# A gated recurrence before an ELU MLP: chunks of 128 tokens with divided decays on half-array matmuls, in place of seven decay levels

## The chip, the cores and the metric

The kernel runs on one core of a Trainium2 chip. Its engines work side by side, each through its own list of instructions in a fixed order: TensorE (PE, with weight loads listed apart as PEld), VectorE (DVE), ScalarE (ACT), GpSimd (POOL) and SyncE (SP), which issues most transfers. The metric is the device time of one execution in microseconds (us). A profile is one such execution, recorded instruction by instruction.

## What is computed

A recurrence over 768 tokens for 4 batches of 8 heads (48 channels each), then an MLP with an ELU in the middle, all in float32. The weights arrive as float64.

```python
f = 1.0 / (1.0 + np.exp(-f_logit))
for t in range(S):
    state = f[:, :, t, :, None] * state + np.einsum('bhd,bhe->bhde', k[:, :, t], v[:, :, t])
    y[:, :, t] = np.einsum('bhd,bhde->bhe', q[:, :, t], state)
# y, with heads side by side, is x: 3072 tokens of 384
h = x @ w_in                                          # 2048 hidden channels
g = np.where(h > 0.0, h, np.exp(np.minimum(h, 0.0)) - 1.0)
out = g @ w_out
```

The gate logits have mean 2 and spread 0.5.

## The kernel before

The work is cut into 12 units of 256 tokens, three to a batch, each of two chunks of 128 tokens. Channels lie on the 128 partitions, two heads to a tile: head 2p in rows 0 to 47, head 2p + 1 in rows 64 to 111, zeros in between; four such pairs stand side by side.

**The recurrence by levels.** Inside a chunk, the score of a query at token i with a key at token j needs the product of all gates between them. `prepare(u)` (lines 171 to 198) turns logits into gates (L174 to L177: clamp, exponential, plus one, reciprocal, each on a 128x1024 tile), and puts the scores of each token with itself on the diagonal of the score tile `at` (L180, L185, L190, L192; `psD` is their PSUM tile). `level(u, l)` (lines 200 to 240) runs seven times per unit. At level l, blocks of 2**l tokens are paired: queries of the odd block meet keys of the even block. ACT copies the queries into a zero-padded tile `qz` (L212), TensorE makes scores of both heads (`psS`, L220), DVE and POOL multiply queries and keys by the next block's product (L230, L231), and DVE copies the scores under a mask into `at` (L233). All factors are products of gates, so none exceeds 1.

`chunk(u, c)` (lines 242 to 293) then makes the outputs: `psY` gets the state's part for both heads in one matmul (L262) and each head's part from `at` (L268, with 48 columns of v as weights). The keys are transposed (`psT`, L255) and multiplied with v into the state's increment `psU` (L276), and DVE carries the state on (L283, L286). ACT copies `psY` to `xt` (L272); six small transfers put the fourth pair's rows into the unused rows of the other three (L293).

**The MLP.** `mlp(u)` (lines 295 to 327) goes through 16 slabs of 128 hidden channels: three matmuls into `psH` (L303), two passes on ACT (L308, L309), one on DVE that finishes the ELU, here called the gate of the slab (L311), and two matmuls into the two `psM` tiles (L318), one slab later. A matmul in float32 stands as two records in the profile.

**The weights.** `weights(n)` (lines 120 to 166) loads one slab as float64 words and makes float32 of it: one pass on ACT (L146) and eight on DVE (L147 to L166), on 128x768 words.

**Order.** The Python program only says which work belongs to which step: MLP steps run two units behind the recurrence, two per level (L334 to L352), and all 16 slabs of weights are converted during units 0 and 1. A scheduler then fixes one order per engine by data dependences and the order of writing. Loads share the SP queue with the small transfers and the outputs.

Of the kernel before, what the change touches and what calls it, by code (L numbers as in the profile page):

```python
# [8 lines left out]
FP32 = mybir.dt.float32  # L9
# [7 lines left out]
def kernel(  # L17
    ctx: ExitStack,
    tc: tile.TileContext,
    q: bass.AP,  # [B, H, D, S]  # L20
    k: bass.AP,  # [B, H, D, S]
    v: bass.AP,  # [B, S, H * D]
    f_logit: bass.AP,  # [B, H, D, S]
    w_in: bass.AP,  # [H * D, DFF]
    w_out: bass.AP,  # [DFF, H * D]
    out: bass.AP,  # [B * S, H * D]
):
    """The gated recurrence, chunk by chunk of 128 tokens, and the ELU MLP on its outputs.

    Inside a chunk the decay between a key at j and a query at i > j is split at the start of the  # L30
    largest power-of-two-aligned block that holds i but not j. At level l (blocks of 2**l tokens)
    the even blocks give keys and the odd blocks queries:
        Q_l[i] = q[i] * prod(f[start of i's block .. i])
        K_l[j] = k[j] * prod(f[j + 1 .. end of j's block])
        T_l[n] = prod(f over block n)
    Each pair (i, j) belongs to exactly one level, and Q_l[i] . K_l[j] is its score. All factors are
    products of gates, so at most 1 in size: nothing is divided by a decay and nothing overflows,
    however small the gates are. Q_7, K_7 and T_7 carry the state from chunk to chunk.

    Channels lie on partitions, two heads to a tile: head 2p in rows 0..47, head 2p + 1 in rows  # L40
    64..111, zeros in between. The weights come as float32, or as the bits of float64 in int64.
    """
    nc = tc.nc
# [23 lines left out]
    # Queries of a level, the two heads of a pair next to each other, each on its own rows.  # L67
# [30 lines left out]
    # masks[l][j, n, w] = 1 where token j lies in block 2n, for the query (2n + 1) * 2**l + w  # L98
# [16 lines left out]
    # The rows of w_in in the order of the rows of xT: heads 2p and 2p + 1 of pair p < NKT, and the  # L115
    # heads of the last pair in the gaps, PAD rows to a gap.
# [212 lines left out]
    def run(steps, n):  # L329
        for _ in range(n):  # L330
            next(steps, None)
# [19 lines left out]
    for u in range(NU - LAG, NU):  # L351
        run(mlp(u), NFT + 2)  # L352
# [32 lines left out]
```

## Time and profile before

| | |
|---|---|
| median of 3 runs | 945.52 us (945.42 to 946.12) |
| span of the profiled execution | 943.6 us |
| TensorE busy | 830.0 us (88%), 4272 matmul records |
| VectorE busy | 543.6 us (58%) |
| ScalarE busy | 324.8 us (34%) |
| GpSimd busy | 186.6 us (20%) |
| bytes read and written in HBM | 31.46 MB, 4.72 MB |

The profiled execution has only its span recorded, 943.6 us; the median of the timed runs lies 1.9 us above it. Busy times of matmuls overlap each other, so distances from start to start tell the pace better than lengths. The chain that ended last gives TensorE 63% of the span, VectorE 16%, and 10% to issue. In a row of groups, the number after the bar is the busy time in us, then the mean of one in ns, then the engine's idle time just before, with what ended it.

### The profile page before, as it was taken

To read this page: it belongs to the slowest core of one execution; us is meant where nothing else is said; L and a number is where in the kernel's file an instruction comes from. 1 tells how busy PE (TensorE), PEld (TensorE's weight loads), DVE (VectorE), ACT (ScalarE), POOL (GpSimd) and SP (SyncE) were. 2 spreads that over 40 slices of the span, in tenths; PEclk is the share of its full clock that TensorE was granted. 3 is DMA by queue.
4 is the path that set the end of the run, shared out by engine and by line. 5 is a ranking of instruction groups with operands and counts; after the bars stand their busy time and mean duration, and the time that the engine had idled before them with its cause. 6 is when DMAs were issued, how large, how long until landed. Compare 5 with 4: busy or idle time off the path is not lost.

```text
span 943.6 us, 11405 instructions
## 1 busy us (share of the span) xinstructions
PE 830.0 (88%) x4272; PEld 644.1 (68%) x4272; DVE 543.6 (58%) x803; ACT 324.8 (34%) x661; POOL 186.6 (20%) x135
## 2 busy tenths in 40 slices
PE   1657657789799899899899899899999999999998
PEld 1555636567587677767777777777787887777775
DVE  8998999999843843742753753753542543421111
ACT  1323232344233433433433433423433433323332
POOL 4521411410310310220220220220211230100000
PEclk9767777999999999989999999989999999999999
DMA  9234514401100200201200200200100000000000
GB/s 219 57 109 110 130 45 124 104 1 46 43 1 22 68 1 21 69 0 26 63 1 19 71 1 18 72 1 17 55 1 3 20 1 22 1 1 22 0 17 17
DMA packets 33527, 38.10 MB, mean 40 GB/s; under 512 B 4160, under 2 KB 31424, under 8 KB 33472
## 3 DMA queue, kind: packets, MB, share of 16 engines
q1 hardware_dynamic: 33472, 37.37, 15.6%
q8 instruction: 34, 0.56, 0.2%
q14 instruction: 21, 0.17, 0.1%
HBM read 31.46 MB, written 4.72 MB: 38 GB/s over the span
## 4 chain that ended last, share of the span: by engine, by line
PE 63%; DVE 16%; issue 10%; POOL 2%; ACT 1%; DMA 1%; DVEq 0%; POOLq 0%; SPq 0%; ACTq 0%
PE psM L318 24%; PE psH L303 20%; PE psS L220 10%; DVE f L177 3%; PE psY L262 3%; PE psY L268 3%; DVE at L233 2%; PE psU L276 2%; DVE q L230 2%; DVE mlo L148 1%; DVE g L311 1%; POOL k L231 1%; DVE ex L158 1%; PE psT L255 1%; DVE ex L155 1%
## 5 line engine op out<-in xcount | busy, mean ns | idle before, releaser
L318 PE MATMUL psM<-wo,g 128*128 128x384 f32 x768 | 296.4, 510 | 35.0 <-DVE g L311 34.8
L303 PE MATMUL psH<-xt,wi 128*128 128x256 f32 x1152 | 286.8, 388 | 0.0
L303 PEld LDWEIGHTS psH<-xt,wi 128*128 128x128 f32 x1152 | 220.0, 196 | 53.9 <-issue 4.2
L318 PEld LDWEIGHTS psM<-wo,g 128*128 128x128 f32 x768 | 147.5, 197 | 105.1 <-DVE g L311 42.2
L220 PEld LDWEIGHTS psS<-qz,k 128*128 128x128 f32 x1344 | 179.8, 208 | 55.7 <-issue 23.1
L220 PE MATMUL psS<-qz,k 128*128 128x128 f32 x1344 | 185.0, 294 | 33.2 <-DVE at L233 18.7
L311 DVE SCALAR_TENSOR_TENSOR g<-e,psH 128x256 f32<-128x256 f32 x192 | 78.9, 416 | 227.4 <-ACT e L309 226.7
L233 DVE COPY_PREDICATED at<-mask,psS 128x512 f32<-128x512 int32 x168 | 144.8, 892 | 76.7 <-PE psS L220 76.5
L231 POOL TENSOR_TENSOR k<-k,tot 128x512 f32<-128x512 f32 x72 | 89.6, 1244 | 396.6 <-PE psS L220 333.5
L212 ACT COPY qz<-q 48x512 f32<-48x512 f32 x168 | 105.8, 630 | 178.3 <-PE psS L220 120.9
L308 ACT ACTIVATE e<-psH 128x256 f32<-128x256 f32 x192 | 73.5, 383 | 260.0 <-PE psH L303 253.0
L309 ACT ACTIVATE e<-e 128x256 f32<-128x256 f32 x192 | 79.9, 416 | 6.0
L177 DVE RECIPROCAL f<-f 128x1024 f32<-128x1024 f32 x12 | 78.5, 6546 | 0.1
L230 DVE TENSOR_TENSOR q<-q,tot 128x512 f32<-128x512 f32 x72 | 56.2, 780 | 3.6 <-ACT qz L212 3.5
L231 POOL TENSOR_TENSOR k<-k,f 128x512 f32<-128x512 f32 x12 | 18.6, 1551 | 199.7 <-PE psS L220 199.7
L262 PE MATMUL psY<-q,state 128*128 128x128 f32 x192 | 47.0, 328 | 9.3 <-DVE q L230 9.3
L185 PE MATMUL psD<-heads,qk 128*128 128x2 f32 x192 | 27.3, 273 | 28.1 <-POOL qk L180 23.4
L192 POOL TENSOR_TENSOR at<-ident,dots 128x2048 f32<-128x2048 f32 x12 | 43.4, 3618 | 38.1 <-ACT dots L190 38.1
L262 PEld LDWEIGHTS psY<-q,state 128*128 128x128 f32 x192 | 30.7, 199 | 24.8 <-issue 14.3
L185 PEld LDWEIGHTS psD<-heads,qk 128*128 128x128 f32 x192 | 27.5, 227 | 28.9 <-POOL qk L180 23.5
L268 PE MATMUL psY<-at,v 128*48 128x128 f32 x384 | 42.9, 303 | 0.7 <-DVE at L233 0.7
L283 DVE TENSOR_TENSOR state<-state,tot 48x192 f32<-48x192 f32 x40 | 15.3, 382 | 46.8 <-PE psY L262 46.3
(45 smaller groups left out, 390.0 us busy)
## 6 DMA issues: line engine op xcount, KB each, us to landing
raw<-in_moe_w_out_dram SPq DMA_DIRECT2D x16, 384.0 KB, 3.6
v<-in_v_dram SPq DMA_DIRECT2D x12, 384.0 KB, 4.9
raw<-in_moe_w_in_dram SPq DMA_DIRECT2D x32, 144.0 KB, 2.8
f<-in_f_logit_dram SPq DMA_DIRECT2D x24, 192.0 KB, 5.4
q<-in_q_dram SPq DMA_DIRECT2D x24, 192.0 KB, 3.4
k<-in_k_dram SPq DMA_DIRECT2D x24, 192.0 KB, 3.5
out_dram<-o SPq DMA_DIRECT2D x24, 192.0 KB, 2.0
raw<-in_moe_w_in_dram SPq DMA_DIRECT2D x32, 48.0 KB, 2.7
```

The source lines that it names most:

```text
L177: nc.vector.reciprocal(f[:], f[:])
L212: nc.scalar.copy(z[HALF[r], :, r, :].rearrange("p a (n w) -> p a n w", w=w), blocks(qt[HALF[r]], 1).rearrange("p (a n) w -> p a n w", n=n),)
L220: nc.tensor.matmul(pc[:, p], lhsT=kt[:, p, c * C : (c + 1) * C], rhs=z[:, p * NCU + c], start=True, stop=True,)
L230: nc.vector.tensor_tensor(out=blocks(qt[:], 1), in0=blocks(qt[:], 1), in1=total(0), op=ALU.mult)
L231: nc.gpsimd.tensor_tensor(out=blocks(kt[:], 0), in0=blocks(kt[:], 0), in1=total(1), op=ALU.mult)
L233: nc.vector.copy_predicated(out=at[:, c].rearrange("p a (n e w) -> p a n e w", e=2, w=w)[:, :, :, 1, :], mask=masks[l][:].unsqueeze(1).bro ...
L262: nc.tensor.matmul(py[:, p, :], lhsT=state[:, p, :], rhs=qt[:, p, cols], start=True, stop=False, skip_group_check=True,)
L303: nc.tensor.matmul(ph[:], lhsT=wi[:, kt, s * 128 : (s + 1) * 128], rhs=x[:, kt, :], start=(kt == 0), stop=(kt == NKT - 1),)
L308: nc.scalar.activation(e[:], ph[:], AF.Relu, scale=-1.0)
L309: nc.scalar.activation(e[:], e[:], AF.Exp, scale=-1.0)
L311: nc.vector.scalar_tensor_tensor(out=g[:], in0=e[:], scalar=-1.0, in1=ph[:], op0=ALU.add, op1=ALU.max)
L318: nc.tensor.matmul(pm[i][:], lhsT=g[:, i * 128 : (i + 1) * 128], rhs=wo[:, s - 1, :], start=(s == 1), stop=(s == NFT),)
```

## The change

The old kernel becomes a function `general` that runs only behind a flag. A new function `fast` does the same work in another way:

- **Divided decays.** With g = 1 + exp(-f_logit), the inverse gate, `prepare` forms the running product of g from the chunk's start (a scan on DVE, L496) and its reciprocal p (L499). Queries are multiplied by p (DVE, L502), keys by the running product (POOL, L503). One set of scores per chunk, set to zero above the diagonal (L529), replaces seven levels and the separate diagonal. Running products grow, so the largest of each chunk is compared with 2**60 (L505).
- **Half-array tiles.** Scores of the two heads use the 48 rows of each head (L524, two PSUM tiles). The increment of the state is made per head with 64 weight columns (L542), outputs with 48 columns (L565), and the state's part with 48 rows and 48 columns (L573). State tiles hold 48 columns per pair.
- **Conversion.** float64 becomes float32 with two passes on ACT (L462, L463), an integer sum on POOL (L471) and four on DVE (L464, L468, and L479 twice on half the words). L479 also turns values that are too small into zero.
- **Order.** The recurrence runs one unit ahead of the MLP, its steps laid out over the 16 slabs; the weights are converted inside the MLP of unit 0, one slab per step, with raw words fetched ahead into three buffers instead of two. `psM` comes two slabs after `psH`.
- **Flag and branch.** Comparisons of all chunks are gathered into one number, every engine loads it behind its last work of `fast` (L694), and `general` runs if any running product passed the limit (L695).

Names in the new lists: `gg` is the ELU's output, `bits`, `rnd` and `sq` are the words of a slab on their way, and `raw4` is the raw words of slab 4.

VectorE's order where weights are converted. Before, two slabs of the opening; the levels of unit 0 stand between their steps:

```order
L158 SCALAR_TENSOR_TENSOR ex2_271<-raw2_263,ex2_271 128x768
L233 COPY_PREDICATED at0_163<-mask5_133,psS0_5_0_355 128x16x32
L162 TENSOR_TENSOR wi_141<-mlo2_270,ex2_271 128x3x128
L166 TENSOR_TENSOR wo_142<-mlo2_270,ex2_271 128x384
L233 COPY_PREDICATED at0_163<-mask5_133,psS0_5_1_360 128x16x32
L147 TENSOR_SCALAR man3_305<-raw3_299 128x768
L151 TENSOR_SCALAR ex3_307<-raw3_299 128x768
L148 SCALAR_TENSOR_TENSOR mlo3_306<-man3_305,mlo3_306 128x768
```

Now, slabs 4 and 5 inside the MLP of unit 0:

```order
L464 TENSOR_SCALAR bits4_404<-raw4_371 128x768
L614 SCALAR_TENSOR_TENSOR gg0_3_464<-e0_3_461,psH0_3_457 128x256
L468 SCALAR_TENSOR_TENSOR bits4_404<-raw4_371,bits4_404 128x768
L479 SCALAR_TENSOR_TENSOR wi_106<-sq4_403,bits4_404 128x3x128
L479 SCALAR_TENSOR_TENSOR wo_107<-sq4_403,bits4_404 128x384
L614 SCALAR_TENSOR_TENSOR gg0_4_504<-e0_4_501,psH0_4_497 128x256
L464 TENSOR_SCALAR bits5_449<-raw5_396 128x768
L468 SCALAR_TENSOR_TENSOR bits5_449<-raw5_396,bits5_449 128x768
L479 SCALAR_TENSOR_TENSOR wi_106<-sq5_448,bits5_449 128x3x128
```

The conversion of a slab stands between the gates of the two slabs before it and of the slab itself, with nothing of a later slab in between; before, it stood among the levels, far ahead of the MLP.

TensorE's order in a later unit. Before, a level, some slabs and the start of a chunk:

```order
L318 MATMUL psM0_1_923<-wo_142,g0_10_1129 128x384
L220 MATMUL psS2_6_0_1166<-qz2_75,k2_71 128x128 x4
L220 MATMUL psS2_6_1_1171<-qz2_75,k2_71 128x128 x4
L303 MATMUL psH0_12_1182<-xt0_471,wi_141 128x256 x3
L318 MATMUL psM0_0_922<-wo_142,g0_11_1140 128x384
L318 MATMUL psM0_1_923<-wo_142,g0_11_1140 128x384
L303 MATMUL psH0_13_1193<-xt0_471,wi_141 128x256 x3
L255 MATMUL psT2_0_1215<-ident_104,k2_71 128x128 x4
L262 MATMUL psY2_0_1223<-q2_70,state0_143 128x128
L268 MATMUL psY2_0_1223<-at2_773,v2_171 48x128 x2
```

Now, the end of unit 3's recurrence inside the MLP of unit 2:

```order
L542 MATMUL psU3_1_1338<-v3_854,kn3_1_1289 64x48 x8
L606 MATMUL psH2_8_1350<-xt2_987,wi_106 128x256 x3
L624 MATMUL psM2_0_1228<-wo_107,gg2_6_1319 128x384
L624 MATMUL psM2_1_1229<-wo_107,gg2_6_1319 128x384
L565 MATMUL psY_104<-at3_1_1258,v3_854 48x128 x8
L573 MATMUL psY_104<-q0_69,state3_0_1245 48x128 x8
L606 MATMUL psH2_9_1388<-xt2_987,wi_106 128x256 x3
```

The pieces of a chunk now stand apart, each between whole slabs, and `psM` uses the gate of two slabs before. The core of the difference:

```diff
+    def convert(n):
+        nc.scalar.activation(rnd[:], lo, AF.Copy, scale=2.0**-29)
+        nc.scalar.activation(sq[:], raw[:].bitcast(FP32)[:, 1::2], AF.Square)
+        nc.vector.tensor_scalar(out=bits[:], in0=hi, scalar1=3, scalar2=0x3FFFFFF8,
+            op0=ALU.logical_shift_left, op1=ALU.bitwise_and)
+        nc.vector.scalar_tensor_tensor(out=bits[:], in0=hi, scalar=-(2**30), in1=bits[:],
+            op0=ALU.bitwise_and, op1=ALU.bitwise_or)
+        nc.gpsimd.tensor_tensor(out=bits[:], in0=bits[:], in1=rnd[:], op=ALU.add)
+        val = bits[:].bitcast(FP32)
+        for o, a, b in ((wi[:, :, n * 128 : (n + 1) * 128], sq[:, 0:DM], val[:, 0:DM]),
+                        (wo[:, n, :].unsqueeze(1), sq[:, DM:], val[:, DM:])):
+            nc.vector.scalar_tensor_tensor(out=o, in0=a..., scalar=(1.125 * 2.0**-15) ** 2,
+                in1=b..., op0=ALU.is_ge, op1=ALU.mult)
...
+    def prepare(u):
+        for h in range(2):
+            nc.scalar.activation(g[:, s], t["f"][:, s], AF.Exp, scale=-1.0)
+            nc.gpsimd.tensor_scalar_add(g[:, s], g[:, s], 1.0)
+            for p in (2 * h, 2 * h + 1):
+                for c in range(NCU):
+                    a = g[:, p, c * C : (c + 1) * C]
+                    nc.vector.tensor_tensor_scan(out=a, data0=a, data1=a, initial=1.0, op0=ALU.mult, op1=ALU.max)
+                    nc.vector.reciprocal(p_[:, p, c * C : (c + 1) * C], a)
+                nc.vector.tensor_tensor(out=t["q"][:, p], in0=t["q"][:, p], in1=p_[:, p], op=ALU.mult)
+                nc.gpsimd.tensor_tensor(out=t["k"][:, p], in0=t["k"][:, p], in1=g[:, p], op=ALU.mult)
...
+    def scores(u, c):
+        for p in range(HP):
+            for r in range(2):
+                nc.tensor.matmul(pc[r][:, p], lhsT=t["k"][HALF[r], p, cols], rhs=t["q"][HALF[r], p, cols], ...)
+        for r in range(2):
+            nc.vector.tensor_tensor(out=at[:, r], in0=pc[r][:], in1=causal[...], op=ALU.mult)
+    def advance(u, c):
+        nc.tensor.matmul(pu[FULL[r], p], lhsT=kns[u, c][:, p, FULL[r]], rhs=vts[u][:, c, h * D : (h + 1) * D], ...)
+    def outputs(u, c):
+        nc.tensor.matmul(py[HALF[r], p, :], lhsT=vts[u][:, c, h * D : (h + 1) * D], rhs=at[:, r, p], ...)
+        nc.tensor.matmul(py[HALF[r], p, :], lhsT=s[HALF[r], p], rhs=t["q"][HALF[r], p, cols], ...)
...
+    def attention(u):
+        return {0: [transposed(u, 0)], 1: [scores(u, 0)], 3: [advance(u, 0)], 4: [scores(u, 1)],
+                5: [] if last else [transposed(u, 1)], 6: [outputs(u, 0)], 8: [advance(u, 1)], 9: [outputs(u, 1)]}
...
+    for m in range(NU):
+        todo = attention(m + 1) if m + 1 < NU else {}
+        steps = prepare(m + 2) if m + 2 < NU else iter(())
+        for s in range(NFT):
+            T = m * NFT + s
+            for f in todo.get(s, ()):
+                f()
+            if m == 0 and ready < NFT:
+                if ready + 1 < NFT:
+                    fetch(ready + 1)
+                convert(ready)
+                ready += 1
+            up(T)
+            if T >= HLAG:
+                down(T - HLAG)
...
+        fast(tc, q, k, v, f_logit, w_in, w_out, out, flag)
+        seen = nc.values_load(flag[0:1, 0:1])
+        with tc.If(seen < 128):
+            general(tc, q, k, v, f_logit, w_in, w_out, out)
```

More of the change, by code (lines that the diff above doesn't have):

```diff
@@ L16, with general @@
 @with_exitstack
-def kernel(
+def general(
     ctx: ExitStack,
@@ L356, with kernel @@
+def kernel(tc, q, k, v, f_logit, w_in, w_out, out):
+    nc = tc.nc
+    with tc.tile_pool(name="flags", bufs=1) as pool:
+        flag = pool.tile([1, 1], I32, name="flag")
+        fast(tc, q, k, v, f_logit, w_in, w_out, out, flag)
+        seen = nc.values_load(flag[0:1, 0:1])
+        with tc.If(seen < 128):
+            general(tc, q, k, v, f_logit, w_in, w_out, out)
 _LAYOUT = {"q": (0, 1, 3, 2), "k": (0, 1, 3, 2), "v": (0, 2, 1, 3), "f_logit": (0, 1, 3, 2)}
```

251 lines of the change are left out of this document (added).

## The prediction

> **What bounds the kernel now.** I read the page's first two parts, then the table by stretches.
>
> ```profile
> span 943.6 us, 11405 instructions
> PE   1657657789799899899899899899999999999998
> DVE  8998999999843843742753753753542543421111
> PEclk9767777999999999989999999989999999999999
> ```
> ```profile
> 0.00:245.00 245.00, 164.94 (x844) 132.17 (x844) 232.28 (x314) 77.81 (x134) 74.99 (x61) 0.83 0.38 95
> 303.83:375.08 71.25, 66.77 (x363) 52.06 (x362) 38.51 (x56) 26.16 (x54) 14.31 (x9) 0.98 0.12 30
> ```
>
> Columns of the table: stretch, length, busy us of PE, PEld, DVE, ACT, POOL, PE clock, DMA share, GB/s. Until 245 us VectorE decides (232 of 245 us busy, PE clock 0.83). Then TensorE does, in a pattern of 71.25 us per unit (256 tokens), PE busy for 66.8. The timeline of PE gives the pace of the MLP alone and of a unit's parts:
>
> ```profile
> 860.39 1.46 PE L303 MATMUL psH<-xt,wi 128*128 128x256 f32 x6
> 861.69 1.45 PE L318 MATMUL psM<-wo,g 128*128 128x384 f32 x4
> 862.98 1.46 PE L303 MATMUL psH<-xt,wi 128*128 128x256 f32 x6
> ```
> ```profile
> 317.83 1.56 PE L318 MATMUL psM<-wo,g 128*128 128x384 f32 x4 [2.53 <-DVE g L311]
> ...
> 324.89 1.95 PE L220 MATMUL psS<-qz,k 128*128 128x128 f32 x16
> 326.68 1.84 PE L185 MATMUL psD<-heads,qk 128*128 128x2 f32 x16
> 330.47 2.61 PE L318 MATMUL psM<-wo,g 128*128 128x384 f32 x4 [1.95 <-DVE g L311]
> ...
> 362.18 0.60 PE L255 MATMUL psT<-ident,k 128*128 128x128 f32 x4
> 362.62 0.39 PE L262 MATMUL psY<-q,state 128*128 128x128 f32 x2
> 362.93 0.42 PE L268 MATMUL psY<-at,v 128*48 128x128 f32 x4
> 363.29 0.49 PE L262 MATMUL psY<-q,state 128*128 128x128 f32 x2
> 363.71 0.42 PE L268 MATMUL psY<-at,v 128*48 128x128 f32 x4
> ...
> 365.61 1.13 PE L276 MATMUL psU<-v,kn 128*128 128x96 f32 x8
> 366.58 1.49 PE L303 MATMUL psH<-xt,wi 128*128 128x256 f32 x6
> ```
>
> Start to start counts here, since ends overlap. A slab (128 hidden channels) takes 862.98 - 860.39 = 2.59 us, a unit of the MLP 16 x 2.59 = 41.4, all twelve 497: the floor that the change leaves alone. Of the other 30 us of a unit, seven levels of 2 x 16 score records (each matmul is two records) take 7 x 2 x 1.79 = 12.5, psU, psY and psT of two chunks some 9, and about 9 are gaps and slow starts like the two marked DVE.
>
> **What goes and what comes, per unit.** Levels, psD, the masked copies and the 1024-wide reciprocal in one piece go. There come, per chunk of 128, four transposes, 8 score matmuls on 48 rows, 8 psU with 64 columns, 8 outputs from `at` on 48 columns, and 8 from the state on 48 rows and 48 columns. Whether two half-array matmuls overlap decides their price. L268 already uses column halves; two narrow timeline windows show its four records:
>
> ```profile
> 652.10 0.32 PE L268 MATMUL psY<-at,v 128*48 128x128 f32 x2
> ```
> ```profile
> 652.25 0.28 PE L268 MATMUL psY<-at,v 128*48 128x128 f32 x2
> ```
>
> Two start together and the other two 0.15 later, so column halves run in pairs. Full-width records are 1.79/16 = 0.111 apart, so a pair costs 0.111. One round of psY (362.93 to 363.71, 0.78) is 2 x 0.111 for L262, two pairs 0.222, and 0.33 for two changes of shape: 0.165 a change. Row halves have no row here: between a pair (0.111 for two) and alone (0.222); nearest is L268, so I take the pair. The psD row bounds psU: 16 records with two columns moved still take the time of 128 columns, so loading 128 weight columns sets 0.11, and 64 columns about half of that. Per chunk:
>
> psT 0.44 (362.18 to 362.62); scores 8 x 0.111 = 0.89 (alone 1.78); psU 8 pairs at about 0.06 = 0.5 (alone 0.9); outputs from `at` 0.89; from the state 0.89 (alone 1.78); seven changes of shape 1.16. Sum 4.8, per unit 9.6. Units 3 to 11 pay this between slabs: 9 x 9.6 = 86, less 3 first chunks without a state (3 x 1.05) and 3 last without psT and psU (3 x 1.3): **79**. Alone in every case it is 130.
>
> **The opening.** The new order runs the recurrence of units 0, 1 and 2, then converts slabs 3 to 15 one by one inside the MLP of unit 0. VectorE's prices:
>
> ```profile
> L177 DVE RECIPROCAL f<-f 128x1024 f32<-128x1024 f32 x12 | 78.5, 6546 | 0.1
> L283 DVE TENSOR_TENSOR state<-state,tot 48x192 f32<-48x192 f32 x40 | 15.3, 382 | 46.8 <-PE psY L262 46.3
> L239 DVE TENSOR_TENSOR tot<-tot 128x256 f32<-128x256 f32 x12 | 5.0, 421 | 2.7 <-POOL k L231 2.7
> L239 DVE TENSOR_TENSOR tot<-tot 128x8 f32<-128x8 f32 x12 | 2.0, 165 | 0.2
> ```
> ```profile
> 56.00 0.94 DVE L158 SCALAR_TENSOR_TENSOR ex<-raw,ex 128x768 int32<-128x768 int32 x1
> ...
> 57.47 0.55 DVE L162 TENSOR_TENSOR wi<-mlo,ex 128x384 f32<-128x384 f32 x1
> ...
> 58.41 0.70 DVE L233 COPY_PREDICATED at<-mask,psS 128x512 f32<-128x512 int32 x1
> ...
> 59.48 0.55 DVE L151 TENSOR_SCALAR ex<-raw 128x768 int32<-128x768 int32 x1
> ```
> ```profile
> L180 POOL TENSOR_TENSOR qk<-q,k 128x1024 f32<-128x1024 f32 x12 | 29.8, 2485 | 16.7 <-DMA q<-in_q_dram 9.3 <-DVE heads L94 7.4
> ```
> ```profile
> 0.80 1.46 SPq L83 DMA_DIRECT2D v<-in_v_dram  x3
> 2.31 0.47 SPq L132 DMA_DIRECT2D raw<-in_moe_w_in_dram  x1
> 5.24 0.81 SPq L78 DMA_DIRECT2D f<-in_f_logit_dram  x2
> ```
> ```profile
> 10.34 1.28 ACT L175 ACT_TABLE_LOAD   x1 [10.34 <-DMA f<-in_f_logit_dram]
> ```
>
> Start: f lands at 10.3 behind three v loads and one of raw, 1.72 MB in 9.5 us. Now one v goes ahead: 0.93 MB, so about 7; then the table 1.3, half an exponential 0.5 and POOL's first sum 0.8 (by L180's rate): VectorE scans from 9.6. One prepare is 8 reciprocals (6546/1024 x 128 + 60 ns = 0.88 each, 7.0), 4 q products (0.42, 1.7) and 8 scans. A scan has no row: 0.17 (128x8) to 0.55 (a 768-wide operation); each element follows the one before, so 0.33, between them: 2.6. Together 11.3. A conversion is 0.55 + 0.94 + 2 x 0.55 = 2.6 on DVE. Up to slab 3's gate: three prepares 34, four conversions 10.4, twelve `at` at 0.70 = 8.4, nine state steps 3.4, four gates 1.7, together 58; plus waits for POOL's sum in each conversion (1.8 less what lies between, 1.4 x 4) and for the last score of a unit (3 x 0.6): 65. So **75 us** there.
>
> From then on VectorE's order is a ring: gate of slab n, two steps of n + 1, wait for POOL's sum, two products; only then can TensorE do psH of n + 1, ACT its two passes, and the next gate run. Nothing of slab n + 2 stands in between. Prices and hand-overs, from the timeline's end, and first a row of the old opening, where twelve psH records took 4.67 us against 12 x 0.216 = 2.6 at full clock:
>
> ```profile
> 105.10 4.67 PE L303 MATMUL psH<-xt,wi 128*128 128x256 f32 x12
> ```
> ```profile
> 937.62 0.42 ACT L309 ACTIVATE e<-e 128x256 f32<-128x256 f32 x1
> 937.65 2.45 PE L318 MATMUL psM<-wo,g 128*128 128x384 f32 x6
> 938.07 0.42 DVE L311 SCALAR_TENSOR_TENSOR g<-e,psH 128x256 f32<-128x256 f32 x1 [2.17 <-ACT e L309]
> 938.54 0.94 PEld L318 LDWEIGHTS psM<-wo,g 128*128 128x128 f32 x4 [0.70 <-DVE g L311]
> ```
>
> Gate 0.42, L464 0.55, L468 0.94, POOL 768/1024 x 2.49 = 1.8, first product 0.55, psH 1.46 at full clock or 2.8 at the slow one (2.0 taken, as the clock was 0.83 in the old opening and PE is now idle more), ACT 0.8, seven hand-overs of 0.05: 7.4. ACT's two conversions (at most 3 x 0.42 each, for three times the width) lie beside the DVE and POOL steps. Ten slabs at 7.4, slab 13 at 4.6 (the order starts its conversion before slab 12's gate), slab 15 at 5.9 up to psH: 84.5. The MLP of unit 1 starts at **160** (bounds 142 and 185: full clock, scans at 0.17 and no waits, or slow clock throughout, scans at 0.55 and 10 us more of waits).
>
> **The sum.** 160 + 1.3 (psM of the last slab) + 11 x 41.4 = 455 + 79 + 9 for what VectorE still holds up (in unit 1 it prepares units 3 to 6 as well: five slabs at 3.4 against 2.59 make 4; clock 2; the rest 3; bounds 0 and 25) + 3.5 (psM's end at 940.1 to the span's end) + 3 for flag and branch, which no row shows (bounds 0 and, as for a load of f, 5.4): 711. The median lies 945.5 - 943.6 = 1.9 above the span: **713 us**. The old gaps of 9 us a unit go because the 6.5 us reciprocal is cut into 0.88 us pieces, below the 2.5 us by which a gate may be late (three blocks of 1.3 until its psH buffer is wanted, less the 1.4 the gate takes). If that cover failed, 9 x 9 = 81 us would come back.
>
> **Rivals.** (1) Row halves do not pair: 130 for 79, 764. For it: no row of this kernel has row halves. Against: column halves pair. (2) Only the state outputs fail to pair, because both heads write the bank psY from different rows: 15 chunks x 0.89 = 13 more, 726. The Trainium skill, TensorEngine Tiling (Array Packing), § Restrictions and Gotchas, says that different row tiles cannot access the same PSUM bank at once; L268's halves share their rows, so no run here shows it yet. (3) A longer opening: slow clock all through adds 0.8 to twelve slabs, and 10 us of waits come before, 733; for it, the old opening's clock slices at 7 and 6. (4) A shorter one: full clock in the ring (12 x 0.54 = 6.5 less), scans at 0.17 (24 x 0.16 = 4 less), none of the 7 us of waits: 695. For it, the ring's longest pause of TensorE is only some 2.6 us. The Trainium skill, TensorE: Matmul & The Clock Gate, § Part 1, lets the clock fall only after an idle window of about 3.4 us, which by itself would make 706; the old opening's slices at 7 and 6 leave that open. (5) The other side, one mechanism: the end branch is taken. It decides at one chunk product of 1 + exp(-f) above 2**60; then the old kernel runs behind the new, 713 + 942 = 1655. Logits of mean 2 and spread 0.5 give 128 x 0.20 = 26 doublings, which speaks against it.
>
> **Chances.** Forecast 0.52, within 690 to 738; (1) 0.11, (2) 0.13, (3) 0.12, (4) 0.08, (5) 0.03, anything else 0.01. The range 686 to 766 takes in all but the branch and part of (1) and (4). A measurement here can tell about 0.2% from no change; only (5) is slower: faster 0.96, same 0.01, slower 0.03.
>
> **What would show it.** Pairs of L524, L542, L565 and L573 starting together and 16 records of L524 in about 0.9 us; one gate every 7.4 us between 75 and 150, VectorE's wait before L479 ended by POOL and before the gate by ACT; psH of unit 1 at about 160; units of 51 us after it; nothing on the branch's far side. Wrong would be a ring at another pace, 1.8 us for 16 scores, or gaps before psM as now.

## The result and the profile after

The changed kernel takes **707.75 us** (median of 4 runs, 707.47 to 709.7) against 945.82 us for the kernel before on the same chip: a ratio of **0.7469**, 95% interval 0.7441 to 0.7497. The forecast was 713 us, 686 to 766. The profiled execution has a span of 706.1 us. First the head of its page:

```profile
span 706.1 us, 9060 instructions
PE   0768844569999999999999999999999999999996
DVE  5889543438852722737124435471226221211110
PEclk9999898789999999999999999999999999999999
```

TensorE is full from about a quarter of the span on, where before it had fives to eights up to slice 9. VectorE is no longer full all through the opening: from slice 6 to 9 it has fours and threes, while TensorE has fours to sixes, so in that stretch no engine is full. The table by stretches says the same (columns as in the prediction: length, busy us of PE, PEld, DVE, ACT, POOL, PE clock, DMA share, GB/s):

```profile
0.00:75.00 75.00, 46.72 (x344) 33.75 (x345) 59.34 (x109) 18.74 (x30) 31.42 (x36) 0.96 0.65 137
75.00:160.00 85.00, 48.87 (x180) 27.13 (x178) 33.58 (x58) 30.80 (x52) 22.32 (x13) 0.87 0.38 105
160.00:205.00 45.00, 44.12 (x165) 32.02 (x166) 36.24 (x79) 17.35 (x42) 19.93 (x20) 0.96 0.53 117
205.00:664.00 459.00, 459.00 (x2589) 333.74 (x2588) 166.19 (x342) 151.04 (x357) 31.79 (x34) 1.00 0.10 29
```

Until 75 us VectorE is the busiest (59 of 75 us); from 75 to 160 no engine is busy for even 60% of the time; from 205 us TensorE has no gap at all. The stretch from 75 to 160 is the ring that the prediction described. One turn of it in VectorE's timeline, from one gate to the next:

```profile
83.60 0.42 DVE L614 SCALAR_TENSOR_TENSOR gg<-e,psH 128x256 f32<-128x256 f32 x1 [2.05 <-ACT e L612]
83.94 0.56 DVE L464 TENSOR_SCALAR bits<-raw 128x768 int32<-128x768 int32 x1
84.53 0.96 DVE L468 SCALAR_TENSOR_TENSOR bits<-raw,bits 128x768 int32<-128x768 int32 x1
87.49 0.56 DVE L479 SCALAR_TENSOR_TENSOR wi<-sq,bits 128x384 f32<-128x384 f32 x1 [2.01 <-POOL bits L471]
87.97 0.55 DVE L479 SCALAR_TENSOR_TENSOR wo<-sq,bits 128x384 f32<-128x384 f32 x1
90.57 0.42 DVE L614 SCALAR_TENSOR_TENSOR gg<-e,psH 128x256 f32<-128x256 f32 x1 [2.05 <-ACT e L612]
```

A turn is 90.57 - 83.60 = 6.97 us, of which VectorE waits 2.01 for POOL's sum and 2.05 for ScalarE. And a unit of TensorE behind the opening, cut to the pieces of the recurrence and what follows each:

```profile
254.54 0.60 PE L513 MATMUL psT<-ident,k 128*128 128x128 f32 x4
254.98 1.46 PE L606 MATMUL psH<-xt,wi 128*128 128x256 f32 x6
...
257.66 1.16 PE L524 MATMUL psS<-q,k 48*128 48x128 f32 x16
258.75 1.56 PE L606 MATMUL psH<-xt,wi 128*128 128x256 f32 x6
...
264.12 0.67 PE L542 MATMUL psU<-v,kn 128*64 128x48 f32 x16
264.72 1.56 PE L606 MATMUL psH<-xt,wi 128*128 128x256 f32 x6
...
274.40 1.08 PE L565 MATMUL psY<-at,v 128*48 128x128 f32 x16
275.41 1.08 PE L573 MATMUL psY<-q,state 48*48 48x128 f32 x16
276.42 1.56 PE L606 MATMUL psH<-xt,wi 128*128 128x256 f32 x6
...
305.39 0.60 PE L513 MATMUL psT<-ident,k 128*128 128x128 f32 x4
```

From psT to the next unit's psT are 305.39 - 254.54 = 50.85 us, where before a unit took 71.25; the MLP's 16 slabs are 41.4 of them.

### The profile page after: what moved, and what is told of

It reads as the page before. It is cut to its first block, busy times and chain, and to the rows that moved or that the text cites. A ratio compares the mean times of both kernels' runs of the same rounds, so it can differ in the third digit from the quotient of the medians.

```text
span 706.1 us, 9060 instructions
## 1 busy us (share of the span) xinstructions
PE 634.7 (90%) x3410; PEld 452.4 (64%) x3410; DVE 300.8 (43%) x599; ACT 229.3 (32%) x509; POOL 105.5 (15%) x102
## 4 chain that ended last, share of the span: by engine, by line
PE 72%; DVE 0%; ACT 0%; issue 0%
PE psH L606 32%; PE psM L624 30%; PE psS L524 3%; PE psY L565 3%; PE psY L573 2%; PE psU L542 1%; PE psT L513 1%; DVE g L496 0%; ACT o L631 0%; DVE gg L614 0%; PE psF L641 0%
## 5 line engine op out<-in xcount | busy, mean ns | idle before, releaser
L624 PE MATMUL psM<-wo,gg 128*128 128x384 f32 x768 | 283.7, 493 | 13.9 <-DVE gg L614 13.8
L614 DVE SCALAR_TENSOR_TENSOR gg<-e,psH 128x256 f32<-128x256 f32 x192 | 79.6, 414 | 320.6 <-ACT e L612 320.5
L624 PEld LDWEIGHTS psM<-wo,gg 128*128 128x128 f32 x768 | 146.3, 192 | 81.5 <-DVE gg L614 19.9
L499 DVE RECIPROCAL p<-g 128x128 f32<-128x128 f32 x96 | 85.2, 920 | 0.3
L503 POOL TENSOR_TENSOR k<-k,g 128x256 f32<-128x256 f32 x48 | 35.0, 746 | 225.4 <-DMA k<-in_k_dram 188.7
L496 DVE TENSOR_TENSOR_SCAN g<-g 128x128 f32<-128x128 f32 x96 | 39.4, 459 | 17.1 <-POOL g L492 17.1
L492 POOL TENSOR_SCALAR g<-g 128x512 f32<-128x512 f32 x24 | 35.4, 1491 | 67.7 <-ACT g L491 67.7
L471 POOL TENSOR_TENSOR bits<-bits,rnd 128x768 int32<-128x768 int32 x16 | 28.9, 1809 | 78.0 <-DVE bits L468 67.0
L524 PEld LDWEIGHTS psS<-q,k 48*128 48x128 f32 x384 | 29.2, 206 | 17.5 <-issue 11.3
L524 PE MATMUL psS<-q,k 48*128 48x128 f32 x384 | 36.5, 313 | 4.0 <-DVE q L502 2.6
L529 DVE TENSOR_TENSOR at<-psS,causal 128x512 f32<-128x512 f32 x48 | 30.9, 681 | 19.8 <-PE psS L524 19.8
L565 PEld LDWEIGHTS psY<-at,v 128*48 128x48 f32 x384 | 21.6, 129 | 13.2 <-issue 6.5
L565 PE MATMUL psY<-at,v 128*48 128x128 f32 x384 | 28.8, 291 | 0.7 <-ACT xt L577 0.7
L573 PE MATMUL psY<-q,state 48*48 48x128 f32 x320 | 22.4, 281 | 0.0
```

The costliest lines, as they stand in the source:

```text
L492: nc.gpsimd.tensor_scalar_add(g[:, s], g[:, s], 1.0)
L496: nc.vector.tensor_tensor_scan(out=a, data0=a, data1=a, initial=1.0, op0=ALU.mult, op1=ALU.max)
L499: nc.vector.reciprocal(p_[:, p, c * C : (c + 1) * C], a)
L503: nc.gpsimd.tensor_tensor(out=t["k"][:, p], in0=t["k"][:, p], in1=g[:, p], op=ALU.mult)
L524: nc.tensor.matmul(pc[r][:, p], lhsT=t["k"][HALF[r], p, cols], rhs=t["q"][HALF[r], p, cols], start=True, stop=True,)
L565: nc.tensor.matmul(py[HALF[r], p, :], lhsT=vts[u][:, c, h * D : (h + 1) * D], rhs=at[:, r, p], start=(p == 0), stop=first, skip_group_chec ...
```

## The experiments

The profiled span, and the ratio to the kernel before, which was measured beside each on the same chip. The runs were made on several chips, so it is the ratios that compare:

| kernel | median us | ratio (95% interval) | span us |
|---|---|---|---|
| changed kernel | 707.75 | 0.7469 (0.7441 to 0.7497) | 706.1 |
| e1 no branch | 703.39 | 0.7433 (0.7400 to 0.7466) | 702.6 |
| e2 halves in turn | 744.19 | 0.7853 (0.7808 to 0.7899) | 743.1 |
| e3 long conversion | 692.84 | 0.7319 (0.7275 to 0.7364) | 690.9 |
| e4 kernel before, short conversion | 940.10 | 0.9926 (0.9897 to 0.9955) | 938.2 |
| e5 slabs ahead | 721.62 | 0.7605 (0.7573 to 0.7637) | 720.0 |
| e6 slabs ahead, long conversion | 710.96 | 0.7491 (0.7460 to 0.7521) | 710.5 |
| e7 one reciprocal | 728.66 | 0.7666 (0.7628 to 0.7705) | 726.8 |
| e8 early flag | 720.34 | 0.7591 (0.7561 to 0.7621) | 718.8 |
| e9 ahead, f first | 688.72 | 0.7259 (0.7216 to 0.7302) | 686.6 |
| e10 ahead, f first, long | 687.02 | 0.7238 (0.7195 to 0.7280) | 683.9 |
| e11 or on VectorE | 695.85 | 0.7327 (0.7296 to 0.7359) | 693.0 |
| e12 ahead, or on VectorE | 683.84 | 0.7201 (0.7169 to 0.7233) | 681.9 |

**e1: the end.**

```diff
-        seen = nc.values_load(flag[0:1, 0:1])
-        with tc.If(seen < 128):
-            general(tc, q, k, v, f_logit, w_in, w_out, out)
```

> Left out: the reading of the range flag and the branch to the general kernel at the end; the flag itself is still worked out, and the order of everything else is unchanged. Theory (the changed kernel's span ends 6.1 us after its last psM, where before it was 3.5 us, and flag and branch make up the difference): 2.6 us less, 705 us for 707.8, and the span ends about 3.5 us after the last psM. Rival (the longer end is the output's transfer, which both kernels have, and the branch lies beside it): no change, 707.8 us, and still 6 us behind the last psM.

Measured: 703.39 us. In the changed kernel ScalarE's last copy starts at 700.04 and the span ends 6.1 us later; here it starts at 699.13 and the span ends 3.5 us later. So reading the flag and branching cost 2.6 us together in these two profiles, as the theory said, and the output's transfer alone, the rival, does not explain the end. (The ratios of the timed runs are too close to settle it by themselves.) The other 0.9 of the 3.5 us between the spans had been lost ahead of unit 3's first psT already (203.79 for 204.71).

**e2: do halves pair?**

```diff
-        for p in range(HP):
-            for r in range(2):
+        for r in range(2):
+            for p in range(HP):
```

(in `scores`, `advance` and twice in `outputs`)

> The same matmuls, but the loops over r and p change places in scores, advance and outputs: four matmuls on one half of the array, then four on the other, so that neighbours in the order share a half. Theory (halves overlap only with a neighbour on the other half): per chunk scores +0.89 us, psU +0.4, outputs from at +0.89, from the state +0.89, 3.07 us in all; 18 chunks of units 3 to 11 lie on the path, less three without a state and three without psU: 18 x 3.07 - 3 x 0.89 - 3 x 0.4 = +51 us, 759 us; 16 records of L524 take 1.8 to 2 us. Rival (a half costs about half of a whole matmul whoever its neighbour is): no change, 708 us, 16 records of L524 in 1.0 to 1.1 us.

Measured: 744.19 us, 37 us more by the spans for the 51 expected. The timeline of TensorE, one chunk's scores and one chunk's outputs:

```profile
268.19 1.71 PE L524 MATMUL psS<-q,k 48*128 48x128 f32 x16
...
286.29 1.55 PE L565 MATMUL psY<-at,v 128*48 128x128 f32 x16
287.77 1.55 PE L573 MATMUL psY<-q,state 48*48 48x128 f32 x16
289.25 1.56 PE L606 MATMUL psH<-xt,wi 128*128 128x256 f32 x6
```

The same 16 records take 1.63 us to the next start instead of 1.09 (scores), 1.48 instead of 1.01 (both kinds of output); psU takes 0.87 instead of 0.60. So the order of the halves decides, and the rival falls. The size was off by a third: four matmuls on one half are 0.111 apart, as pairs are, but where the half changes the first matmuls of the new half run beside the last ones of the old, and the change of shape is paid either way. Twice 1.75 us a chunk explains the unit (54.37 for 50.85); unit 3's first psT comes 7.5 us later as well (212.18 for 204.71), and the two together make the 37.

**e3: the old conversion in the new kernel.**

```diff
-        nc.scalar.activation(rnd[:], lo, AF.Copy, scale=2.0**-29)
-        nc.scalar.activation(sq[:], raw[:].bitcast(FP32)[:, 1::2], AF.Square)
...
-        nc.gpsimd.tensor_tensor(out=bits[:], in0=bits[:], in1=rnd[:], op=ALU.add)
...
+        nc.scalar.activation(mlo[:], lo, AF.Copy, scale=2.0**-52, bias=1.0)
+        nc.vector.tensor_single_scalar(out=man[:], in_=hi, scalar=0x000FFFFF, op=ALU.bitwise_and)
...
+        nc.vector.tensor_tensor(out=wo[:, n, :], in0=mlo[:, DM:], in1=scale[:, DM:], op=ALU.mult)
```

(lines 146 to 166 of the kernel before in place of lines 459 to 482)

> The changed kernel with the old eight-step conversion of a slab on VectorE, without POOL's sum and without the two passes of ACT for it (one in their place). VectorE's work per slab goes from 2.6 to 5.9 us. Theory (from 75 to 160 us a ring of waits through VectorE, TensorE and ACT sets the pace, of which VectorE's own work is less than half; in this order the first four steps of the next slab stand ahead of the gate, where VectorE waits anyhow): gates 6.3 to 7.4 us apart for 6.94 now, and up to slab 3 four conversions at +1.9 us: between -1 and +15 us, 707 to 723 us. Rival (the opening is VectorE's work and every microsecond of it counts, as in the kernel before): 16 x 3.3 = +53 us, 761 us, with VectorE's waits in the ring as long as now.

Measured: **692.84 us, 15 us faster** than with the short conversion. Both forecasts missed: the rival's sign, and the theory's range. VectorE's timeline in the ring's place:

```profile
106.85 0.41 DVE L617 SCALAR_TENSOR_TENSOR gg<-e,psH 128x256 f32<-128x256 f32 x1
107.19 0.55 DVE L473 TENSOR_SCALAR ex<-ex 128x768 int32<-128x768 int32 x1
107.77 0.96 DVE L476 SCALAR_TENSOR_TENSOR ex<-raw,ex 128x768 int32<-128x768 int32 x1
...
109.24 0.55 DVE L485 TENSOR_TENSOR wo<-mlo,ex 128x384 f32<-128x384 f32 x1
109.71 0.55 DVE L465 TENSOR_SCALAR man<-raw 128x768 int32<-128x768 int32 x1
...
111.98 0.42 DVE L617 SCALAR_TENSOR_TENSOR gg<-e,psH 128x256 f32<-128x256 f32 x1
```

A turn takes 5.13 us here with no wait in it: the scheduler put four steps of the next slab (L465 to L470) ahead of the gate, where they fill the time of psH and ScalarE. The eight steps are 4.8 us start to start (107.19 to 111.98), not the 5.9 of the expectation; that alone had put my lower bound of 6.3 too high. Twice the work on VectorE beats half of it here, because the half comes with two waits.

**e4: the short conversion in the old kernel.**

```diff
-        nc.scalar.activation(mlo[:], lo, AF.Copy, scale=2.0**-52, bias=1.0)
...
+        nc.scalar.activation(rnd[:], lo, AF.Copy, scale=2.0**-29)
+        nc.scalar.activation(sq[:], raw[:].bitcast(FP32)[:, 1::2], AF.Square)
...
+        nc.gpsimd.tensor_tensor(out=bits[:], in0=bits[:], in1=rnd[:], op=ALU.add)
...
```

(the same exchange the other way round, in `weights`)

> The kernel before with one part of the change alone: the shorter conversion, with its two ACT passes and POOL's sum. Theory (the old opening is VectorE's work: 232 of 245 us busy): 16 x 3.3 = 53 us less work, of which the wait for POOL's sum gives back up to 1.4 us a slab: between -53 and -30 us, 893 to 916 us for 945.8. Rival (the old opening waits on the levels and on POOL's products, and the conversion fills gaps): within 5 us of 945.8.

Measured: 940.10 us, a ratio 0.7% below one, or some 7 us; the theory's 30 to 53 us did not come, and the rival's 5 us are missed by a little. Groups of VectorE up to 245 us, in this kernel and, second, in the kernel before:

```profile
L228 DVE TENSOR_TENSOR q<-q,tot 128x512 f32<-128x512 f32 x22 | 22.4, 1020 | 0.1
L161 DVE SCALAR_TENSOR_TENSOR wi<-sq,bits 128x384 f32<-128x384 f32 x16 | 14.3, 894 | 14.8 <-POOL bits L153 14.8
```
```profile
L230 DVE TENSOR_TENSOR q<-q,tot 128x512 f32<-128x512 f32 x22 | 18.6, 846 | 0.1
L162 DVE TENSOR_TENSOR wi<-mlo,ex 128x384 f32<-128x384 f32 x16 | 9.0, 562 | 0.0
```

Three things take it back: 14.8 us of waits for POOL's sum; instructions that grow (the product into `wi` from 562 to 894 ns, the untouched query products from 846 to 1020 ns); and, since VectorE's busy time up to 245 us still falls from 232.28 to 209.66 us, other waits, of which those for TensorE (psY, psS and psU) grow from 5.0 to 13.0 us.

**e5, e6: break the ring by fetching the slabs ahead.** Six raw buffers, fetched six ahead on ScalarE's queue; e6 with the long conversion as well.

```diff
-            nc.sync.dma_start(out=di[64 * r : 64 * r + D], in_=main[r])
+            nc.scalar.dma_start(out=di[64 * r : 64 * r + D], in_=main[r])
...
-    AHEAD = 3
+    AHEAD = 6
...
-                if ready + 1 < NFT:
-                    fetch(ready + 1)
+                if ready + 4 < NFT:
+                    fetch(ready + 4)
```

> The changed kernel with its short conversion, but the raw slabs are fetched six ahead into six buffers, on ScalarE's queue of transfers instead of SyncE's. With that the order lets VectorE do the steps of later slabs ahead of the gates that it has to wait for, and part of unit 3's recurrence moves into the opening too. Theory (the 6.94 us from gate to gate are waits in a ring, made by the order; VectorE's own work per slab is 2.5 us start to start and 0.35 for the gate): TensorE reaches the MLP of unit 1 at 125 to 135 us instead of 160, 672 to 685 us. Rival 1 (what sets the pace is a resource, the slabs' transfers or POOL's sum with its 1.8 us of which it slows VectorE): at least as long as the long conversion in the same kernel, 690 to 708 us, with VectorE's steps well over their 0.55 and 0.95 us. Rival 2 (the shorter opening is used up by waits in unit 1): MLP of unit 1 earlier, but unit 3's first psT not.

> The same with the old eight-step conversion. In the run with the long conversion alone VectorE is busy for 63 of the 70 us from 75 to 145, so there is little for another order to win: theory (with the ring gone VectorE's work counts, 4.6 us start to start for the long conversion and 2.5 for the short one): 684 to 693 us, 12 to 38 us behind the short conversion in the same order. Rival (the short conversion is no gain in any order, since POOL's sum has to be waited for or slows VectorE): level with or ahead of the short one.

Measured: 721.62 and 710.96 us. The first is slower than the changed kernel, the second level with it (0.7460 to 0.7521 against 0.7441 to 0.7497); no expectation named these times, though the long conversion is ahead of the short one, as e6's rival said. The timeline of ScalarE in e5:

```profile
40.02 1.28 ACT L491 ACT_TABLE_LOAD   x1 [40.02 <-DMA raw<-in_moe_w_out_dram]
```

The table load, at 7.74 us in the changed kernel, comes at 40.02: thirty transfers stand ahead of it in ScalarE's order, and it issues them at the pace at which transfers go through, not at 0.45 us each. f had been issued at 1.76 us on SyncE's queue and was not what was waited for (the expectation of e9 below still says that f landed late; that was my misreading). The 32 us at the start hide what the broken ring gives, so this pair does not test the ring; e9 does.

**e7: the reciprocal in one piece.**

```diff
-                    nc.vector.reciprocal(p_[:, p, c * C : (c + 1) * C], a)
+        nc.vector.reciprocal(p_[:], g[:])
```

(the new line stands behind the loop over the scans)

> The changed kernel with one reciprocal of 1024 columns per unit (6.5 us) in place of eight of 128 (0.92 us each), behind the unit's scans. Theory (a gate may be late by 2.5 us before TensorE stops; a 6.5 us instruction ahead of it makes it late by up to 6.5): some 4 us of idle TensorE in each unit's MLP in which one is prepared, units 1 to 9, less about 1 us a unit that is saved in the opening: 707.8 + 9 x 4 = 744, from 730 to 750 us. Rival (the gates have slack enough, since the recurrence between the slabs gives TensorE other work): 703 to 709 us.

Measured: 728.66 us, 21 us more, which is neither. The table by stretches of this kernel shows where:

```profile
160.00:205.00 45.00, 34.02 (x158) 24.79 (x159) 36.21 (x56) 15.31 (x34) 19.02 (x18) 0.89 0.51 99
...
260.00:664.00 404.00, 403.89 (x2275) 292.36 (x2274) 145.71 (x252) 130.79 (x309) 26.68 (x28) 1.00 0.09 26
```

Up to slab 15's psH 5.2 us are lost (it starts at 165.51 for 160.36). From 160 to 205 us TensorE is idle for 11.0 us, 4.0 of them still in the ring, where in the changed kernel it is idle for 0.9. In unit 1's MLP late gates do stop it, as the theory says. First VectorE's timeline, then TensorE's:

```profile
189.44 6.55 DVE L503 RECIPROCAL p<-g 128x1024 f32<-128x1024 f32 x1
195.91 0.68 DVE L615 SCALAR_TENSOR_TENSOR gg<-e,psH 128x256 f32<-128x256 f32 x2
...
196.32 2.93 PE L607 MATMUL psH<-xt,wi 128*128 128x256 f32 x6 [4.53 <-DVE gg L615]
```

Scans stand ahead of this piece as well (4.54 us from 184.86 on). From 160 to 262 us psH waits for a gate four times, 8.4 us in all; in the changed kernel it waits once, for 0.5 us. The scheduler also moved unit 3's first psT into this stretch (175.06 for 204.71), so the order differs by more than the piece. But from 260 us on TensorE is idle for 0.11 of 404 us, though the 6.55 us pieces stand there too, one of them right ahead of gates:

```profile
300.29 6.55 DVE L503 RECIPROCAL p<-g 128x1024 f32<-128x1024 f32 x1
306.75 0.68 DVE L615 SCALAR_TENSOR_TENSOR gg<-e,psH 128x256 f32<-128x256 f32 x2
```

Two gates run back to back at 306.75, the first some 5 us behind the end of its pass on ScalarE (301.82), and TensorE does not stop. What this kernel loses, it loses ahead of 260 us: the theory's mechanism holds in unit 1's MLP, and the rival's slack in the units behind it.

**e8: the flag read early.** On top of e5:

```diff
+        if m == NU - 2:
+            seen = nc.values_load(flag[0:1, 0:1])
```

> As the run with the slabs fetched ahead and the short conversion, but the engines read the range flag into their registers behind the eleventh unit's MLP, where it has long been worked out, and only the comparison and the branch are left at the end. Theory (the 2.6 us at the end are the reading of the flag, which all engines wait for): 2 to 2.6 us less than that run. Rival (they are the branch itself and what it fetches): the same time as that run, or more, if the reading holds TensorE up in the middle.

Measured: 720.34 us for e5's 721.62, which the ratios do not tell apart, and the end is about as long as in e5 (the last copy starts at 712.83, the span ends at 718.8: 6.0 us for 6.3). But ScalarE and SyncE still read the flag behind their last work, at 712.8 and 713.7: the scheduler moved the reading back there. The run does not tell reading from branching; it is inconclusive.

**e9, e10: the same, with the first three slabs on SyncE's queue again.** Six buffers; slabs 0 to 2 as in the changed kernel, the later ones on ScalarE's queue behind unit 0's exponentials; e10 with the long conversion.

```diff
-            nc.sync.dma_start(out=di[64 * r : 64 * r + D], in_=main[r])
+            (nc.sync if n < 3 else nc.scalar).dma_start(out=di[64 * r : 64 * r + D], in_=main[r])
...
     convert(1)
+    for n in range(AHEAD, AHEAD + 3):
+        fetch(n)
```

> Again the short conversion with slabs fetched six ahead into six buffers, but the first three slabs go on SyncE's queue behind f, k and q as in the changed kernel, and only the later ones on ScalarE's, whose first comes behind unit 0's exponentials. In this order the first two steps of slab n + 2 stand ahead of the gate of slab n, so POOL's sum has a whole slab's time. Theory (in the run with all slabs on ScalarE's queue f landed some 32 us late, and that alone made it slow; the 6.94 us are the ring): unit 0's scans from about 11 us again, gates about 3 to 4 us apart behind slab 3, MLP of unit 1 at 115 to 130, 663 to 680 us. Rival 1 (slabs come at the rate of the transfers: 0.79 MB at the 102 to 139 GB/s of the stretches now are 5.7 to 7.7 us a slab): gates 5.7 us apart or more, VectorE's idle time ended by DMA raw, 690 to 708 us. Rival 2 (POOL's sum slows VectorE or is itself late): gates 5 us apart or more with waits for POOL bits, 680 to 700 us.

> The same with the long conversion. Theory (VectorE's work, 4.6 us start to start and 0.35 for the gate, sets the pace, in this order as in the run with the long conversion alone): gates 5 to 6 us apart, 685 to 695 us, behind the short conversion by 10 us or more. Rival (the short conversion is no gain in any order): level with or ahead of it.

Measured: 688.72 and 687.02 us. Both beat the changed kernel by about 20 us, so the ring was worth breaking; but e9 misses its theory's 680, and the short conversion is again no better than the long one, as e10's rival said. Two reasons show in e9's timeline, of VectorE and POOL first, then of ScalarE:

```profile
78.50 1.80 POOL L471 TENSOR_TENSOR bits<-bits,rnd 128x768 int32<-128x768 int32 x1 [2.95 <-DVE bits L468]
78.61 2.12 DVE L479 SCALAR_TENSOR_TENSOR wi<-sq,bits 128x384 f32<-128x384 f32 x1
...
40.50 0.63 ACT L491 ACTIVATE g<-f 128x512 f32<-128x512 f32 x1 [14.96 <-DMA raw<-in_moe_w_in_dram]
```

The product into `wi` takes 2.12 us instead of 0.55: it starts 0.11 behind POOL's sum and ends 0.43 behind the sum's end. L468 took 2.42 us in the same place at 84.89, for 0.96. That is a full stop for as long as this sum runs. The Trainium skill, SBUF — State Buffer, § Summary: rules for kernel authors, says so: a VectorE instruction with two SBUF inputs and a GpSimd instruction that reads SBUF exclude each other, and the later one waits until the first is done. The trace agrees for this sum. It does not for POOL's other one, of one input (L492): at 105.62 the same product starts when that has 1.42 us left and takes 0.96. And unit 1's exponential waits until 40.50 behind ScalarE's own transfers, so the first gate runs at 60.35 us (51.20 in the changed kernel).

**e11: no POOL in the conversion.** The low bits are joined by an or on VectorE.

```diff
-        nc.scalar.activation(rnd[:], lo, AF.Copy, scale=2.0**-29)
+        nc.scalar.activation(rnd[:], lo, AF.Copy, scale=2.0**-29 * (1 - 2.0**-9), bias=-0.49)
-        nc.gpsimd.tensor_tensor(out=bits[:], in0=bits[:], in1=rnd[:], op=ALU.add)
+        nc.vector.tensor_tensor(out=bits[:], in0=bits[:], in1=rnd[:], op=ALU.bitwise_or)
```

> The changed kernel with its short conversion, but POOL's sum of the low bits is replaced by an or on VectorE (768 wide, two inputs, 0.96 us by L468); so that nothing carries, ScalarE rounds the low word down instead of to the nearest, which leaves out at most one unit of the last place of a float32 weight. POOL has no part in the conversion any more. Theory (the ring costs 6.94 us, 2 of which are the wait for POOL's sum and the hand-overs to it and back; in this order the ring stays): gates about 1.1 us closer, 5.85 us, over some 12 slabs 13 us less, and in the opening 4 x 1 us less: 690 to 695 us, level with the long conversion in the same kernel. Rival (POOL's part is no loss; the order alone made the long conversion faster): 703 us or more.

Measured: 695.85 us, 12 us less than the changed kernel. A turn of its ring:

```profile
97.97 0.42 DVE L614 SCALAR_TENSOR_TENSOR gg<-e,psH 128x256 f32<-128x256 f32 x1 [2.05 <-ACT e L612]
...
99.96 0.96 DVE L471 TENSOR_TENSOR bits<-bits,rnd 128x768 int32<-128x768 int32 x1
...
104.10 0.42 DVE L614 SCALAR_TENSOR_TENSOR gg<-e,psH 128x256 f32<-128x256 f32 x1 [2.05 <-ACT e L612]
```

6.13 us instead of 6.97 (5.85 expected): the wait for POOL is gone, the one for ScalarE stands. The time lies 0.9 us outside the theory's range, but the mechanism holds; the rival falls.

**e12: both.** The fetching of e9 with the or of e11.

> The same or on VectorE in the kernel with slabs fetched ahead and f first, in which two steps of a later slab stand ahead of each gate. Theory (in that kernel the short conversion was no better than the long one, because VectorE's two-input instructions beside POOL's sum took up to 2.4 us instead of 0.55 or 0.96, and because the gate waits for that sum): with POOL out, 3.3 us of VectorE's work per slab and 0.35 for the gate, gates 3.5 to 4.5 us apart once three of them are done; 670 to 682 us for 688.7 and 687.0. Rival (there the later start, from transfers that go ahead, and ScalarE's queue set the pace, whichever the conversion): 684 to 690 us.

Measured: **683.84 us**, the fastest of all, 3.6% below the changed kernel by the ratios (0.7201 / 0.7469) and 28% below the one before. It is 4.9 us faster than e9, and 3.2 faster than e10, but not below 682. Its interval (0.7169 to 0.7233) touches e9's (0.7216 to 0.7302) and reaches into e10's (0.7195 to 0.7280), so the gain over the sum on POOL is small, and against the long conversion the difference is not settled. One thing that holds it back shows in ScalarE's timeline:

```profile
100.14 0.91 ACT L462 ACTIVATE rnd<-raw 128x768 int32<-128x768 uint32 x1 [3.92 <-DMA raw<-in_moe_w_in_dram]
```

ScalarE stands behind its own transfers for 3.92 us here, and VectorE's or for this slab waits 3.55 us for it. So the time lies between theory and rival: taking POOL out gives 4.9 us here for the theory's 7 to 19. That ScalarE's queue is the next bound is likely from this row, but not shown: a version that issues the slabs from elsewhere was not tried.

## Why the prediction was right, point by point

**The start (75 us to slab 3's gate): 77.24 measured.** The table load began at 7.74 (about 7 forecast). The groups show two prices that were too low:

```profile
L492 POOL TENSOR_SCALAR g<-g 128x512 f32<-128x512 f32 x24 | 35.4, 1491 | 67.7 <-ACT g L491 67.7
L496 DVE TENSOR_TENSOR_SCAN g<-g 128x128 f32<-128x128 f32 x96 | 39.4, 459 | 17.1 <-POOL g L492 17.1
```

POOL's sum of one input takes 1.49 us for 0.8, so VectorE scans from 11.28 instead of 9.6; a scan takes 0.46 for 0.33, inside its bounds (0.17 to 0.55; 0.39 where POOL is quiet, by the records of the trace). The reciprocals were priced right (0.92 on the mean for 0.88).

**The ring (7.4 us a slab, slab 15's psH and with it the MLP of unit 1 at 160): 6.97 a turn, and slab 15's psH at 160.36.** Its parts and waits are those forecast: VectorE waits for POOL ahead of L479 and for ScalarE ahead of the gate. It is shorter mainly because psH ran mostly at full clock (1.56 us for the 2.0 taken); VectorE's instructions that wait for nothing also start up to 0.08 us before the one ahead has ended by the profile. Not in all of the stretch, though, as TensorE's timeline shows:

```profile
111.86 1.56 PE L624 MATMUL psM<-wo,gg 128*128 128x384 f32 x4 [1.38 <-DVE gg L614]
116.20 1.85 PE L606 MATMUL psH<-xt,wi 128*128 128x256 f32 x6 [2.78 <-DVE wi L479]
119.43 2.93 PE L624 MATMUL psM<-wo,gg 128*128 128x384 f32 x4 [1.38 <-DVE gg L614]
123.43 2.93 PE L606 MATMUL psH<-xt,wi 128*128 128x256 f32 x6 [1.07 <-DVE wi L479]
```

Blocks of 1.56 us take 2.93 here, behind pauses of 2.78 us at most; the clock granted from 118.1 to 130.5 us is 0.50. The Trainium skill, TensorE: Matmul & The Clock Gate, § Part 1, which lets the clock fall only after an idle window of about 3.4 us, agrees with the slabs at full clock and not with these; what sets the clock here stays open. Turns with slow blocks take 8.31 us, and the ten turns forecast at 7.4 take 7.36 on the mean: the 2.0 us for psH lay between the two clocks and stood for both. That 160.36 meets 160 so closely is luck in part: slab 3's gate is 2.2 us late, and slab 15's psH follows the gate before it in 4.9 us for the 5.9 forecast.

**Behind the opening (1.3 + 455 + 79 + 9 = 544.3 us): 539.6**, from 160.36 to 700.0, where the last psM ends. The recurrence costs 50.85 - 41.4 = 9.5 us a unit for the 9.6 forecast, row by row: psT 0.44, scores 1.09 (0.89 and a change of shape of 0.165), psU 0.60 (0.5 and 0.165), both outputs 1.01 each (0.89 and 0.165; they follow each other without a gap). The other 1.2 us of a unit lie in the slabs beside them, whose blocks grow from 1.3 to 1.4 us. Halves pair, the state's outputs too, though their two heads write one bank: rivals (1) and (2) fall. Rival (1) was also priced too high: its 130 takes every half alone, and row halves alone would add 18 x 0.89 + 15 x 0.89 = 29 us, 742 in all. The sentence that (2) takes from the Trainium skill, TensorEngine Tiling (Array Packing), § Restrictions and Gotchas, does not hold here, where the two heads differ in rows and in columns. The term that was mis-sized is the 9 us for what VectorE still holds up: 539.6 leaves 4.3 for it, and TensorE is idle for 0.9 of the 45 us from 160 to 205, at a granted clock of 0.96, and for nothing after it.

**The end (3.5 + 3): 6.1**, and e1 gives the second part as 2.6. The branch was not taken; rival (5) did not come. Nor did (3) and (4): the granted clock from 75 to 160 us is 0.87, neither half nor full all through.

**The cover of the reciprocal: right in outcome, its reason only in part.** I wrote that the old gaps of 9 us a unit go because the reciprocal is cut into pieces shorter than the 2.5 us by which a gate may be late, and that 81 us would come back without that. In e7 it is in one piece, and 21 us come back, nearly all ahead of 260 us. In unit 1's MLP late gates do stop TensorE there, for 8.4 us; behind it a gate some 5 us late stops nothing, so for those units 2.5 us was too small a slack and 81 us too high a price. The order of the new `fast`, in which psM uses the gate of two slabs before and the recurrence's pieces stand between slabs, has more slack than I counted. That this slack is what removed the old gaps is argued, not shown: no run took it away.

**What was not seen: one part of the change costs time.** I priced the short conversion's steps correctly, and never asked what the long one would take in the new order. By the ratios, the new recurrence with the old conversion is 0.7319, the old recurrence with the new conversion 0.9926, both together 0.7469: the recurrence and its order bring some 254 us, and the conversion gives 15 us of them back (e3). Its sum on POOL is most of that in this order: without it e11 is 12 us faster.

## What to carry to other kernels

Price a shortened step in the order in which it will stand: where engines hand work around in a ring, fewer instructions on one of them gain nothing if they bring another hand-over, and more work may cost nothing if it can stand ahead of a wait, as in e3. Look for stretches in which no engine is busy, and break the order there; but what issues the earlier loads must not be an engine that the start waits for. Half-array matmuls give most of their gain only if neighbours in the order lie on different halves (e2).

## What the runs showed of the hardware

- Matmuls on halves of the array run two at a time in whichever direction they are split, rows, columns or both, if the order alternates: 16 records of 48x48 tiles in 1.01 us, against 1.48 us with four matmuls of one half in a row (e2); 1.09 against 1.63 for row halves, 0.60 against 0.87 for column halves of 64.
- A VectorE instruction with two inputs in SBUF that starts during POOL's sum of two inputs (L471) ends only after it: 2.12 us for 0.55, 2.42 for 0.96 (e9). So does L464, which has one, in the same trace: 2.12 for 0.55 at 121.77. Beside POOL's sum of one input (L492) the wait is shorter than that: 0.96 for 0.55 with 1.42 us of it left. Instructions that read PSUM keep their time beside POOL (`at` 0.67 beside, 0.68 alone), and so do reciprocals (0.92 both ways), by the records of that trace.
- An engine that issues transfers can be held by them: ScalarE issued its first four 0.5 us apart, but needed 40 us for 30 (e5), and nothing else of its list ran meanwhile.
- Reading a flag and a branch not taken at the end of the program cost 2.6 us together (e1).
- TensorE's blocks took 2.93 us for 1.56, at a granted clock of 0.50, with no pause above 2.8 us ahead of them in the ring (the changed kernel, 118 to 131 us).
